# Two weight loads made whole, x loaded in two halves, and the final copy and store split over two engines and two queues, in a one-core decode layer

## The chip, the cores and the metric

The kernel runs on one core of one Trainium2 chip. The metric is the device time of one execution in microseconds (us). Lower is better. Single executions of the kernel before ran from 138.02 to 138.56 us, so differences below 0.3% need several executions, and each comparison below used 5 or 6 of the tried kernel and 6 to 11 of the kernel before, on the same chip. Different experiments ran on different chips.

A ratio in this document is the mean time of one kernel's runs divided by the mean of the other's from the same rounds, with a 95% interval in brackets. It is therefore not quite the ratio of the medians that are quoted beside it.

## The reference

One decode step of a transformer layer, for a batch of 4 with one token each, in bf16:

```python
x = A_x                                   # (4, 1, 1024)
h = x + attn(layernorm(x))                # wq 1024x4096, KV cache: last 2048 of 8192 positions,
                                          # 32 query heads, 4 KV heads, Dh 128; wo 4096x1024
h2 = h + (silu(n @ w1) * (n @ w3)) @ w2   # n = layernorm(h); w1, w3 1024x3584, w2 3584x1024
return h2
```

Almost all the bytes are weights and cache: wq 8.4 MB, K and V 8.4 MB each, wo 8.4 MB, and w1, w3 and w2 7.3 MB each, together 55.6 MB that must come from HBM once.

## The kernel before

All big loads go through one queue (SyncE's) into one ring of SBUF memory, in a fixed plan. Each load is issued as soon as the program order and the ring space allow it. The scheduler of the kernel language places the semaphore waits. This is the part that the change touches, with cuts marked:

```python
plan = [
    ("wq", load_rows, (0, wq_v, N_Q, 0, 4)),            # first half of wq
    ("wq", load_rows, (32 * KIB, wq_v, N_Q, 4, 4)),     # second half
    ("k", ...), ("k", ...), ("v", ...), ("v", ...), ("wo", ...), ("w1", ...),
    ("w3", load_rows, (0, w3_v, N_F, 0, 4)),            # first half of w3
    ("w3", load_rows, (28 * KIB, w3_v, N_F, 4, 4)),     # second half
    ("w2", ... 17 rows), ("w2", ... 7), ("w2", ... 3), ("w2", ... 1),
]
nc.scalar.dma_start(out=x_sb[:], in_=x_flat)            # x, 4 rows of 2 KB, ScalarE's queue
# ... cut: four more small loads of x in another layout (x_q), ScalarE's queue
# ... cut: layer norm, q = x wq, K transposes and scores, softmax, PV, wo
for i in range(IO):                                     # wo, 32 rows
    # ... matmuls of row i
    if i == 11:
        load_next()                                     # second half of w3
# ... cut: layer norm, w1, silu, w3
for i in range(IF):                                     # w2 accumulates on h in y2_ps (one PSUM bank)
    # ... 4 matmuls of row i
res = act.tile([P, CG], BF16)                           # 128 x 256
nc.scalar.copy(out=res[:], in_=y2_ps[:])
nc.scalar.dma_start(out=out_flat.rearrange("b (j c) -> j b c", j=JG), in_=res[0:P:RS, :])
```

## Time and profile before

| | before |
|---|---|
| median device time (first three runs) | 138.23 us (138.06 to 138.29) |
| span in the profile | 136.3 us |
| bytes read from HBM | 55.59 MB |
| share of the span in which the load queue's packets keep the 16 DMA engines busy | 95.3% |
| TensorE (PE) busy | 50% |

The slice table cuts the span into 40 slices of 3.4 us; each digit is the busy share of the DMA engines in tenths.

```profile
DMA  5999899999999999997988989989799999989960
```

The load stream has no hole from about 3 us to 133 us. The chain that ended last, followed back from the end, says the same by engine and by line:

```profile
DMA 58%; PE 21%; ACT 13%; DVE 5%; issue 1%; SPq 0%; ACTq 0%
DMA ring<-in_B_w_dram 42%; DMA ring<-in_A_wq_dram 16%; PE kt_ps L263 9%; ACT kT L269 6%; PE scores_ps L248 5%; ACT z L304 3%; PE q_ps L215 2%; PE g_ps L403 2%; DVE rmax L280 2%; ACT Pm L285 2%; PE OT_ps L326 2%; DVE pT L294 1%; DVE z L300 1%; ACT L285 1%; DVE q_sb L225 1%
```

Now the timeline. The columns are start in us, length in us, engine, line, operation, output and inputs, shape, count, and in brackets the idle time before it and what ended it. A name ending in q (ACTq, SPq) is an engine's sequencer, here issuing a DMA. First the start of the kernel:

```profile
2.52 1.27 DVE L158 BATCH_NORM_STATS2 stats<-x_sb 4x6 f32<-4x512 bf16 x2
...
13.05 3.58 PE L215 MATMUL q_ps<-ring,xnT 128*4 128x512 bf16 x32 [6.05 <-DMA ring<-in_A_wq_dram]
...
22.55 3.15 PE L215 MATMUL q_ps<-ring,xnT 128*4 128x512 bf16 x32 [5.92 <-DMA ring<-in_A_wq_dram]
...
27.45 2.03 PE L263 MATMUL kt_ps<-ident,ring 128*128 128x128 bf16 x33
```

The first half of wq lands and 32 matmuls run at 13.05; the other 32 run at 22.55, when the second half is there. Then K starts. Here is the rest of the weights and the tail:

```profile
107.50 3.13 PE L403 MATMUL u_ps<-ring,hnT 128*32 128x448 bf16 x32 [3.00 <-DMA ring<-in_B_w_dram]
...
115.98 3.17 PE L403 MATMUL u_ps<-ring,hnT 128*32 128x448 bf16 x32 [5.34 <-DMA ring<-in_B_w_dram]
...
120.33 1.70 DVE L425 STREAM_TRANSPOSE hgT<-hg 128x896 bf16<-128x896 bf16 x1
...
126.30 3.82 PE L433 MATMUL y_ps<-ring,hgT 128*32 128x256 bf16 x68 [7.14 <-DMA ring<-in_B_w_dram]
...
132.38 0.92 PE L433 MATMUL y_ps<-ring,hgT 128*32 128x256 bf16 x16 [0.71 <-DMA ring<-in_B_w_dram]
...
133.35 0.37 ACT L443 CAST res<-y_ps 128x256 bf16<-128x256 f32 x1 [26.54 <-PE y_ps L433]
133.75 0.61 ACTq L444 DMA_DIRECT2D out_dram<-res  x1
```

Every weight matmul is released by a load ("<-DMA"). Between the end of hgT (122.0) and the first w2 load (126.3) there are 4.3 us of slack. After the last load comes the only part that nothing hides: four matmuls, a 0.37 us copy, a store.

### The profile page before, as it was taken

To read this page: it belongs to the slowest core of one execution; us is meant where nothing else is said; L and a number is where in the kernel's file an instruction comes from. 1 tells how busy PE (TensorE), PEld (TensorE's weight loads), DVE (VectorE), ACT (ScalarE), POOL (GpSimd) and SP (SyncE) were. 2 spreads that over 40 slices of the span, in tenths; PEclk is the share of its full clock that TensorE was granted. 3 is DMA by queue.
4 is the path that set the end of the run, shared out by engine and by line. 5 is a ranking of instruction groups with operands and counts; after the bars stand their busy time and mean duration, and the time that the engine had idled before them with its cause. 6 is when DMAs were issued, how large, how long until landed. Compare 5 with 4: busy or idle time off the path is not lost.

```text
span 136.3 us, 2302 instructions
## 1 busy us (share of the span) xinstructions
PE 67.9 (50%) x1035; PEld 42.9 (31%) x1035; DVE 42.6 (31%) x73; ACT 31.0 (23%) x36; POOL 1.7 (1%) x8
## 2 busy tenths in 40 slices
PE   0101803698989889105259538830096440900960
PEld 0100201274656565001149427610043210300840
DVE  6440000244444444609940030160000695070000
ACT  0400000155555646092944000000003300000001
POOL 5000000000000000000000000000000000000000
PEclk9999999999999999965555865897557777555577
DMA  5999899999999999997988989989799999989960
GB/s 156 462 462 443 385 413 418 423 447 423 428 437 409 437 437 423 435 582 341 538 385 365 524 365 442 459 353 522 328 412 463 434 437 447 429 388 409 426 261 5
DMA packets 2662, 55.75 MB, mean 409 GB/s; under 512 B 312, under 2 KB 344, under 8 KB 604
## 3 DMA queue, kind: packets, MB, share of 16 engines
q1 hardware_dynamic: 2592, 55.58, 95.3%
q8 instruction: 8, 0.13, 0.3%
q10 hardware_dynamic: 60, 0.02, 0.1%
q14 instruction: 2, 0.02, 0.0%
HBM read 55.59 MB, written 0.01 MB: 408 GB/s over the span
## 4 chain that ended last, share of the span: by engine, by line
DMA 58%; PE 21%; ACT 13%; DVE 5%; issue 1%; SPq 0%; ACTq 0%
DMA ring<-in_B_w_dram 42%; DMA ring<-in_A_wq_dram 16%; PE kt_ps L263 9%; ACT kT L269 6%; PE scores_ps L248 5%; ACT z L304 3%; PE q_ps L215 2%; PE g_ps L403 2%; DVE rmax L280 2%; ACT Pm L285 2%; PE OT_ps L326 2%; DVE pT L294 1%; DVE z L300 1%; ACT L285 1%; DVE q_sb L225 1%
## 5 line engine op out<-in xcount | busy, mean ns | idle before, releaser
L269 ACT COPY kT<-kt_ps 128x1024 bf16<-128x1024 bf16 x16 | 15.8, 1014 | 12.0 <-PE kt_ps L263 12.0
L263 PE MATMUL kt_ps<-ident,ring 128*128 128x128 bf16 x256 | 16.4, 219 | 0.0
L263 PEld LDWEIGHTS <-ring 128*128 128x128 bf16 x256 | 14.3, 98 | 5.0 <-issue 4.9
L267 DVE COPY kT<-kt_ps 128x1024 bf16<-128x1024 bf16 x16 | 11.1, 691 | 15.2 <-PE kt_ps L263 15.2
L215 PE MATMUL q_ps<-ring,xnT 128*4 128x512 bf16 x64 | 6.7, 596 | 12.0 <-DMA ring<-in_A_wq_dram 12.0
L403 PEld LDWEIGHTS <-hnT 128*32 128x32 bf16 x128 | 5.3, 137 | 23.1 <-issue 20.5
L248 PE MATMUL scores_ps<-kT,qz 128*32 128x512 bf16 x64 | 9.9, 609 | 3.1 <-ACT kT L269 3.1
L326 PE MATMUL OT_ps<-z,ring 128*128 128x32 bf16 x256 | 7.4, 185 | 6.7 <-ACT z L304 5.0
L403 PE MATMUL u_ps<-ring,hnT 128*32 128x448 bf16 x64 | 6.3, 572 | 8.3 <-DMA ring<-in_B_w_dram 8.3
L403 PE MATMUL g_ps<-ring,hnT 128*32 128x448 bf16 x64 | 5.4, 525 | 9.0 <-DMA ring<-in_B_w_dram 9.0
L433 PE MATMUL y_ps<-ring,hgT 128*32 128x256 bf16 x112 | 5.7, 370 | 8.4 <-DMA ring<-in_B_w_dram 8.3
L326 PEld LDWEIGHTS <-ring 128*128 128x128 bf16 x256 | 7.3, 103 | 7.4 <-issue 7.4
L433 PEld LDWEIGHTS <-hgT 128*32 128x32 bf16 x112 | 4.4, 129 | 10.3 <-issue 6.1
L215 PEld LDWEIGHTS <-xnT 128*4 128x4 bf16 x64 | 2.1, 116 | 16.2 <-issue 15.9
L353 PE MATMUL y_ps<-ring,o 128*32 128x256 bf16 x128 | 5.8, 365 | 2.0 <-DMA ring<-in_A_wo_dram 2.0
L443 ACT CAST res<-y_ps 128x256 bf16<-128x256 f32 x1 | 0.4, 372 | 26.5 <-PE y_ps L433 26.5
L304 ACT ACTIVATE z<-pt_ps,mask 128x512 bf16<-128x512 f32 x8 | 5.3, 687 | 3.5 <-DVE z L300 3.5
L225 DVE TENSOR_SCALAR q_sb<-q_ps 128x512 bf16<-128x512 f32 x1 | 0.7, 690 | 17.2 <-PE q_ps L215 17.2
L353 PEld LDWEIGHTS <-o 128*32 128x32 bf16 x128 | 4.8, 130 | 3.8 <-issue 3.1
L300 DVE TENSOR_SCALAR z<-pt_ps,mask 128x512 bf16<-128x512 f32 x8 | 5.5, 740 | 1.2 <-ACT z L304 0.8
L296 PE MATMUL pt_ps<-pT,perm 128*128 128x512 bf16 x4 | 2.4, 607 | 6.8 <-DVE pT L294 6.8
L417 DVE RECIPROCAL eg<-eg 128x896 f32<-128x896 f32 x1 | 5.8, 5753 | 0.0
(73 smaller groups left out, 40.5 us busy)
## 6 DMA issues: line engine op xcount, KB each, us to landing
ring<-in_A_wq_dram SPq DMA_DIRECT2D x2, 4096.0 KB, 16.8
ring<-in_A_k_cache_dram SPq DMA_DIRECT2D x4, 2048.0 KB, 25.5
ring<-in_A_v_cache_dram SPq DMA_DIRECT2D x4, 2048.0 KB, 40.2
ring<-in_B_w_dram SPq DMA_DIRECT2D x1, 7168.0 KB
ring<-in_B_w_dram SPq DMA_DIRECT2D x2, 3584.0 KB, 28.6
ring<-in_B_w_dram SPq DMA_DIRECT2D x1, 4352.0 KB
ring<-in_B_w_dram SPq DMA_DIRECT2D x1, 1792.0 KB
ring<-in_B_w_dram SPq DMA_DIRECT2D x1, 768.0 KB
```

Of the source, the lines that this page charges most:

```text
L215: nc.tensor.matmul(q_ps[QD * g : QD * g + B, hf * 512 : (hf + 1) * 512], lhsT=xnT[:, kc, :], rhs=wq_t[:, c0 : c0 + 512], start=(kc == 0), ...
L248: nc.tensor.matmul(scores_ps[QD * g : QD * (g + 1), n * 512 : (n + 1) * 512], lhsT=qz[:, b, g * QD : (g + 1) * QD], rhs=kT_v[:, g, :, :], ...
L263: nc.tensor.transpose(out=kt_ps[:, jj, :], in_=k_v[:, n * NJ + t * TB + jj, :], identity=ident[:])
L267: nc.vector.tensor_copy(out=kT[:, t * TB : (t + 1) * TB, :], in_=kt_ps[:])
L269: nc.scalar.copy(out=kT[:, t * TB : (t + 1) * TB, :], in_=kt_ps[:])
L300: nc.vector.tensor_scalar(out=z[:, :, g, :], in0=pt_ps[:], scalar1=mask[:, g : g + 1], scalar2=None, op0=ALU.mult)
L304: nc.scalar.mul(out=z[:, :, g, :], in_=pt_ps[:], mul=mask[:, g : g + 1])
L326: nc.tensor.matmul(OT_ps[:, b, :], lhsT=loaded["v"][b][:, j, :], rhs=PTz[j // NJ][:, (j % NJ) * B + b, :, :], start=(j == 0), stop=(j == J ...
L353: nc.tensor.matmul(y_ps[QD * j : QD * (j + 1), :], lhsT=o4[:, i, :, :].rearrange("p b s -> p (b s)"), rhs=loaded["wo"][i][:, j * CG : (j + ...
L403: nc.tensor.matmul(out_ps[QD * j : QD * (j + 1), hf, :HF], lhsT=hnT[:, k, :], rhs=loaded[kind][k][:, c0 : c0 + HF], start=(k == 0), stop=( ...
L417: nc.vector.reciprocal(out=eg[:], in_=eg[:])
L433: nc.tensor.matmul(y2_ps[QD * j : QD * (j + 1), :], lhsT=hgT[:, i, :], rhs=loaded["w2"][i][:, j * CG : (j + 1) * CG], start=False, stop=(i ...
```

## The change

The intent: fewer and larger loads for wq and w3, and a shorter tail, by splitting the last copy over VectorE and ScalarE by columns and storing each part from its own queue. x is also loaded as two column halves, so that the layer norm statistics can begin on the first. The core of the diff:

```diff
-        ("wq", load_rows, (0, wq_v, N_Q, 0, 4)),
-        ("wq", load_rows, (32 * KIB, wq_v, N_Q, 4, 4)),
+        ("wq", load_rows, (0, wq_v, N_Q, 0, 8)),
 ...
-        ("w3", load_rows, (0, w3_v, N_F, 0, 4)),
-        ("w3", load_rows, (28 * KIB, w3_v, N_F, 4, 4)),
+        ("w3", load_rows, (0, w3_v, N_F, 0, 8)),       # issued after wo's row 12
 ...
-    nc.scalar.dma_start(out=x_sb[:], in_=x_flat)
+    for c0, c1 in ((0, 512), (512, D)):
+        nc.scalar.dma_start(out=x_sb[:, c0:c1], in_=x_flat[:, c0:c1])
 ...
-    nc.scalar.copy(out=res[:], in_=y2_ps[:])
-    nc.scalar.dma_start(out=out_flat.rearrange("b (j c) -> j b c", j=JG), in_=res[0:P:RS, :])
+    out_v = out_flat.rearrange("b (j c) -> j b c", j=JG)
+    CV = 160
+    nc.vector.tensor_copy(out=res[:, :CV], in_=y2_ps[:, :CV])
+    nc.scalar.copy(out=res[:, CV:], in_=y2_ps[:, CV:])
+    nc.sync.dma_start(out=out_v[:, :, :CV], in_=res[0:P:RS, :CV])
+    nc.scalar.dma_start(out=out_v[:, :, CV:], in_=res[0:P:RS, CV:])
```

(The calls that issue the next load were moved to fit; they are cut here.)

More of the change, by code (lines that the diff above doesn't have):

```diff
@@ L136 @@
     x_sb = act.tile([B, D], BF16)
-    nc.scalar.dma_start(out=x_sb[:], in_=x_flat)
-    load_next(5)
+    for c0, c1 in ((0, 512), (512, D)):
+        nc.scalar.dma_start(out=x_sb[:, c0:c1], in_=x_flat[:, c0:c1])
+    load_next(4)
     ident = const.tile([P, P], BF16)
@@ L221 @@
                 )
-        if kc == RQ - 1:
-            load_next()
+    load_next()
     q_sb = act.tile([P, CQ], BF16)
@@ L332 @@
             )
-        if b % BS == BS - 1:
+        if b == BS - 1:
             load_next()
```

## The prediction

> **What bounds the kernel now.** The load stream. The profile's slice table shows the DMA engines 8 to 10 tenths busy from 3 to 133 us; the windows view gives 426 to 430 GB/s in the wq and K stages. In the timeline the weight matmuls start when loads land: wq halves at 13.05 and 22.55 us, wo 82.25, w1 99.06, w3 halves 107.50 and 115.98, w2 126.30, 130.55, 132.38, 133.0. Then come four matmuls, a 0.37 us ScalarE copy and the store (issue 0.61 us), ending at 136.3.
>
> **What the change does.**
>
> 1. Bytes, and so stream time, stay the same. One load instead of two saves about 0.4 us of issue, already hidden. Gain: 0.
>
> 2. wq whole: the 32 matmuls that ran at 13.05 (3.58 us) now wait until 22.5. All 64 take about 6.4 us, to 28.9 (before 25.7). In the built order 16 K transposes now precede the q transposes, hiding the q copies: K starts at about 29, not 27.45. K, softmax and PV come 1.5 to 3 us later. w1's load is issued when half of PV is done: 73.2 becomes 75 to 76. The queue has wo to move until about 80 (lands 82.25, less an estimated 2 us of completion), so it stays fed. The third K load now waits for all of wq (22.5, not 13.05); two K loads (10 us) are queued by then.
>
> 3. PV's result comes at about 83 instead of 81; wo matmuls (5.8 us) and layer norm (4.2 us) end at about 94, still ahead of w1 at 99.
>
> 4. w3 whole is issued after wo's row 12, at 85 to 87; w1 keeps the queue busy to about 97. But all 64 w3 matmuls start at about 116 and take 5.4 to 6.3 us (before: 3.17 us after the second half). hg and hgT (1.09, 1.70 us) end at about 125 instead of 122.05; w2's first piece lands at 126.3. 1 to 2 us of 4.2 us slack are left.
>
> 5. Final copy: in the built program ScalarE's part waits for VectorE's. Both read one PSUM bank (the Trainium skill, "PSUM — Partial Sum Buffer", section on bank collisions, says engines can't access one bank of a partition in the same cycle; no run here shows that yet). Estimate from the trace's copies (VectorE 0.29 us at 128 columns, 0.42 at 256; ScalarE 0.27 and 0.37): 0.32 + 0.05 + 0.24 = 0.61 us against 0.37. The second store is issued 0.2 us later, and the second queue gains nothing (the skill, "DMA: Bandwidth & Descriptors", "Issuing engines are not separate DMA queues": all run on the same 16 engines). Cost: +0.2 us.
>
> **On the critical path** lies only point 5; 2 to 4 eat slack. From 138.23 us I predict 138.4 us, range 137.9 to 139.3. Faster by over 2%: 2%; within 2%: 95%; slower: 3%.
>
> **What would show it.** Right: last w2 landing at 133 us, give or take 0.4; no hole in the DMA share; q matmuls one block of about 6.4 us from 22.5; w3 matmuls one block at 116; w2 matmuls released by the load; ScalarE's res copy after VectorE's. Wrong: a hole in the load stream near 80 or 97 us (2, 4); the first w2 matmul released by hgT (4); the copies overlapping (5).
>
> **What would make it wrong.** A lower granted TensorE clock (0.5 in many windows after 62 us) stretching PV or the w3 block beyond their slack; stores under 512 bytes a row (320 and 192) completing more slowly; a different load rate with 64 KB rows per partition than with 32 KB.

## More of the kernel before

The store's packets, in the DMA view of the window from 134.4 to 135.45 us, are 20 packets on ScalarE's queue (q10) and nothing else:

```profile
DMA  0000000000000000000000022221000000000000
...
q10 hardware_dynamic: 20, 0.01, 2.9%
```

## The result, and the profile after

| | before | after |
|---|---|---|
| median device time | 138.19 us (138.04 to 138.40, 6 runs) | 138.94 us (138.75 to 139.17, 6 runs) |
| ratio | | 1.0055, 95% interval 1.0041 to 1.0068 |
| span in the profile | 136.3 us | 137.0 us |

The change costs 0.75 us. That lies inside the predicted range (137.9 to 139.3) and counts as "within 2%", but the predicted cost was only 0.2 us. The rest of this document is about the other 0.55 us.

The slice table and the chain after. The stream is as full as before:

```profile
DMA  9797996999999999999979999989989989997940
```

```profile
DMA 56%; PE 25%; ACT 11%; DVE 4%; issue 1%; ACTq 0%; SPq 0%
DMA ring<-in_B_w_dram 40%; DMA ring<-in_A_wq_dram 16%; PE kt_ps L261 10%; PE scores_ps L246 6%; ACT kT L267 5%; PE q_ps L214 5%; ACT z L302 3%; PE g_ps L401 2%; DVE rmax L278 2%; ACT Pm L283 2%; PE OT_ps L324 1%; DVE pT L292 1%; DVE z L298 1%; ACT L283 1%; PE qt_ps L227 1%
```

The start after the change, as a timeline:

```profile
10.44 0.68 DVE L157 BATCH_NORM_STATS2 stats<-x_sb 4x6 f32<-4x512 bf16 x1 [7.41 <-DMA x_sb<-in_A_x_dram]
...
22.68 6.44 PE L214 MATMUL q_ps<-ring,xnT 128*4 128x512 bf16 x64 [9.54 <-DMA ring<-in_A_wq_dram]
...
29.05 0.84 PE L261 MATMUL kt_ps<-ident,ring 128*128 128x128 bf16 x12
```

The 64 matmuls of wq now form one block of 6.44 us at 22.68, and K starts at 29.05 instead of 27.45. A surprise off the critical path: the statistics of x's second half start only at 10.44 us, because that 4 KB load had not landed before. The tail after the change:

```profile
82.70 1.65 PE L324 MATMUL OT_ps<-z,ring 128*128 128x32 bf16 x55 [4.15 <-issue]
...
86.15 5.46 PE L351 MATMUL y_ps<-ring,o 128*32 128x256 bf16 x128 [0.82 <-DVE o L340]
...
99.12 5.35 PE L401 MATMUL g_ps<-ring,hnT 128*32 128x448 bf16 x64 [5.46 <-DMA ring<-in_B_w_dram]
...
116.05 5.43 PE L401 MATMUL u_ps<-ring,hnT 128*32 128x448 bf16 x64 [11.57 <-DMA ring<-in_B_w_dram]
...
122.65 1.70 DVE L423 STREAM_TRANSPOSE hgT<-hg 128x896 bf16<-128x896 bf16 x1
...
126.31 3.82 PE L431 MATMUL y_ps<-ring,hgT 128*32 128x256 bf16 x68 [4.83 <-DMA ring<-in_B_w_dram]
...
132.37 0.90 PE L431 MATMUL y_ps<-ring,hgT 128*32 128x256 bf16 x16 [0.76 <-DMA ring<-in_B_w_dram]
...
133.32 0.32 DVE L443 CAST res<-y_ps 128x160 bf16<-128x160 f32 x1 [8.97 <-PE y_ps L431]
133.67 0.69 SPq L445 DMA_DIRECT2D out_dram<-res  x1
133.68 0.24 ACT L444 CAST res<-y_ps 128x96 bf16<-128x96 f32 x1 [26.89 <-DVE res L443]
134.08 0.62 ACTq L446 DMA_DIRECT2D out_dram<-res  x1
```

The w3 matmuls are one block from 116.05, hgT ends at 124.35, and the w2 matmuls are still released by the load, at 126.31 (before: 126.30), and the last 16 at 132.37 (before: 132.38). So in these profiles everything up to the last load takes the same time. The whole difference comes after it. ScalarE's copy starts only after VectorE's has ended. And in the DMA view of the same window as before, something new is in the way:

```profile
DMA  0000000000009000000000111000000000001100
...
q14 instruction: 1, 0.01, 3.1%
q1 hardware_dynamic: 20, 0.01, 2.1%
q10 hardware_dynamic: 15, 0.00, 1.2%
```

Queue q14 is an instruction queue: one packet of instructions (8,192 bytes, 525 ns in the packet records) runs at 134.74 us, and the stores' packets (q1 and q10) run from 134.97 us.

The tail can be read as a sum of four terms, worked out from the packet and semaphore records of each trace and from the device time of the profiled run: A from the end of the last load packet to the issue of the last store; B from there until that store has landed; C from there to the end of the span; D the device time less the span. In us:

```text
kernel                  last load    A     B     C     D    sum A..D   device
before                   132.67    1.08  1.75  0.84  1.78    5.45     138.12
after                    132.60    1.47  2.05  0.84  1.87    6.23     138.83
```

This sum is better to compare than single times: in seven profiles of kernels whose loads are those of the kernel before, the end of the last load packet varied from 132.67 to 132.98 us, while the sum of a second profile of the kernel before came out at 5.42. The change added 0.39 in A, 0.30 in B and 0.09 in D. Only about 0.24 of A was predicted.

### The profile page after: what moved, and what is told of

Its sections match the earlier page's. It is cut to its first block, busy times and chain, and to the rows that moved or that the text cites. A ratio compares the mean times of both kernels' runs of the same rounds, so it can differ in the third digit from the quotient of the medians.

```text
span 137.0 us, 2303 instructions
## 1 busy us (share of the span) xinstructions
PE 67.0 (49%) x1035; PEld 42.0 (31%) x1035; DVE 42.7 (31%) x74; ACT 31.0 (23%) x36; POOL 1.7 (1%) x8
## 4 chain that ended last, share of the span: by engine, by line
DMA 56%; PE 25%; ACT 11%; DVE 4%; issue 1%; ACTq 0%; SPq 0%
DMA ring<-in_B_w_dram 40%; DMA ring<-in_A_wq_dram 16%; PE kt_ps L261 10%; PE scores_ps L246 6%; ACT kT L267 5%; PE q_ps L214 5%; ACT z L302 3%; PE g_ps L401 2%; DVE rmax L278 2%; ACT Pm L283 2%; PE OT_ps L324 1%; DVE pT L292 1%; DVE z L298 1%; ACT L283 1%; PE qt_ps L227 1%
## 5 line engine op out<-in xcount | busy, mean ns | idle before, releaser
L261 PE MATMUL kt_ps<-ident,ring 128*128 128x128 bf16 x256 | 17.1, 220 | 0.0
L246 PE MATMUL scores_ps<-kT,qz 128*32 128x512 bf16 x64 | 10.5, 609 | 2.6 <-ACT kT L267 2.6
L401 PE MATMUL u_ps<-ring,hnT 128*32 128x448 bf16 x64 | 5.4, 523 | 11.6 <-DMA ring<-in_B_w_dram 11.6
L171 PE MATMUL tp_ps<-ident,xn 4*128 4x4 bf16 x8 | 0.7, 199 | 12.5 <-DVE xn L164 12.5
```

The costliest lines, as they stand in the source:

```text
L246: nc.tensor.matmul(scores_ps[QD * g : QD * (g + 1), n * 512 : (n + 1) * 512], lhsT=qz[:, b, g * QD : (g + 1) * QD], rhs=kT_v[:, g, :, :], ...
L261: nc.tensor.transpose(out=kt_ps[:, jj, :], in_=k_v[:, n * NJ + t * TB + jj, :], identity=ident[:])
L401: nc.tensor.matmul(out_ps[QD * j : QD * (j + 1), hf, :HF], lhsT=hnT[:, k, :], rhs=loaded[kind][k][:, c0 : c0 + HF], start=(k == 0), stop=( ...
```

## The experiments

Theory at first: all of the 0.75 us lies in the copies and stores, and the loads cost nothing. Rival: the whole loads, with their larger packets, cost part of it.

### Only the loads changed

```diff
  (wq, w3 and x_sb loaded as in the changed kernel; final copy and store as before)
```

> The changed loads (wq, w3, x_sb) with the old final copy and single store. Theory T (all of the +0.75 us lies after the last load): 138.1 to 138.3 us, ratio 1.000 give or take 0.001; last w2 landing at 133.0. Rival L (whole wq and w3, or their 64 KB and 56 KB packets, cost part of it): 138.45 us or more, with the last landing or the last w2 matmul later than in the kernel before.

Measured: 138.62 us against 138.12; ratio 1.0026 (1.0012 to 1.0041). Something in the load part costs about 0.36 us (difference of the means), which the theory did not allow. But the sum of its tail is 5.68, not 5.45, although its tail's code is that of the kernel before. The last load packet ended at 132.81, within the spread of the other profiles, so the later landing that the rival named is not seen.

### Only the tail changed

```diff
-    nc.scalar.copy(out=res[:], in_=y2_ps[:])
-    nc.scalar.dma_start(out=..., in_=res[0:P:RS, :])
+    (two copies and two stores, as in the changed kernel)
```

> The loads of the kernel before with the new final copies and two stores. Theory T: 138.85 to 139.05 us, ratio 1.0045 to 1.006, all of the change's cost. Rival L: clearly less, 138.3 to 138.6.

Measured: 138.51 us against 138.12; ratio 1.0025 (1.0011 to 1.0039). So the tail costs about 0.39 us, and the first theory fell: the tail alone is not all, and the two halves of the change add up to the whole (0.36 + 0.39 against 0.75). Its timeline:

```profile
133.64 0.32 DVE L445 CAST res<-y_ps 128x160 bf16<-128x160 f32 x1 [11.31 <-PE y_ps L433]
133.99 0.69 SPq L447 DMA_DIRECT2D out_dram<-res  x1
134.00 0.24 ACT L446 CAST res<-y_ps 128x96 bf16<-128x96 f32 x1 [26.98 <-DVE res L445]
134.26 0.61 ACTq L448 DMA_DIRECT2D out_dram<-res  x1
```

ScalarE's copy waits for VectorE's, as predicted. Its store is issued 0.03 us after its copy ends (before rounding). In the changed kernel that gap was 0.16 us, with the same code.

### Within the tail: two copies, one store

```diff
-    nc.scalar.copy(out=res[:], in_=y2_ps[:])
+    nc.vector.tensor_copy(out=res[:, :160], in_=y2_ps[:, :160])
+    nc.scalar.copy(out=res[:, 160:], in_=y2_ps[:, 160:])
     nc.scalar.dma_start(out=out_v, in_=res[0:P:RS, :])
```

> Split copies (VectorE, then ScalarE waiting for it), then one store of whole 512-byte rows from ScalarE's queue. Theory C: store issued 0.3 to 0.35 us later, 138.5 to 138.6. If C were all of it: 138.9. If the serial copies cost nothing: 138.2.

Measured: 138.40 us against 138.12; ratio 1.0018 (1.0005 to 1.0030), 0.24 us by the means.

```profile
133.48 0.33 DVE L445 CAST res<-y_ps 128x160 bf16<-128x160 f32 x1 [11.43 <-PE y_ps L433]
133.84 0.24 ACT L446 CAST res<-y_ps 128x96 bf16<-128x96 f32 x1 [27.89 <-DVE res L445]
134.11 0.61 ACTq L447 DMA_DIRECT2D out_dram<-res  x1
```

The copies take 0.60 us from the start of the first to the end of the second, against 0.37 before, and term A grows from 1.08 to 1.30. This is the part of the cost that the prediction named, at its predicted size (0.24 us). The run's own expectation, a store 0.3 to 0.35 us later, was too high: A grew by 0.2 us.

### Within the tail: one copy, two stores

```diff
     nc.scalar.copy(out=res[:], in_=y2_ps[:])
-    nc.scalar.dma_start(out=..., in_=res[0:P:RS, :])
+    nc.sync.dma_start(out=out_v[:, :, :160], in_=res[0:P:RS, :160])
+    nc.scalar.dma_start(out=out_v[:, :, 160:], in_=res[0:P:RS, 160:])
```

> One ScalarE copy as before, then the two column stores (320 and 192 bytes a row) from two queues. Theory S (the second store and the narrow rows cost about half, as the longer time from last packet to completion in the profile suggests): 138.4 to 138.7. Rival C (only the serial copies cost): 138.2.

Measured: 138.62 us against 138.12; ratio 1.0032 (1.0019 to 1.0045), 0.44 us by the means.

```profile
133.52 0.37 ACT L445 CAST res<-y_ps 128x256 bf16<-128x256 f32 x1 [27.53 <-PE y_ps L433]
133.91 0.69 SPq L446 DMA_DIRECT2D out_dram<-res  x1
133.92 0.61 ACTq L447 DMA_DIRECT2D out_dram<-res  x1
```

Both stores are issued at the same moment, no later than before, yet term B is 2.08 instead of 1.75: two stores issued together complete later than one. The packet records show where: ScalarE's packets move from 135.17 to 135.29 us, 1.25 us after the issue as in the kernel before, and SyncE's only from 135.53, after them. SyncE's queue is not slow by itself: in tail_only, where its store was issued first, it landed 1.77 us after its issue. Term C is 0.94 instead of 0.84; its cause comes up below.

### Two stores by rows

```diff
     nc.scalar.copy(out=res[:], in_=y2_ps[:])
-    nc.scalar.dma_start(out=..., in_=res[0:P:RS, :])
+    nc.sync.dma_start(out=out_v[0:2], in_=res[0:64:RS, :])      # every row keeps 512 bytes
+    nc.scalar.dma_start(out=out_v[2:4], in_=res[64:P:RS, :])
```

> One ScalarE copy as before, two stores from two queues, split by rows, so that every row keeps its 512 bytes. Theory R (rows under 512 bytes are what made the two column stores cost 0.44 us): 138.1 to 138.3. Rival Q (a second store costs by itself, through its second issue and completion): 138.4 to 138.6.

Measured: 138.55 us against 138.21; ratio 1.0024 (1.0012 to 1.0036), 0.32 us by the means; term B 1.97, term C again 0.94. The second store costs by itself, without narrow rows: about 0.2 us in B and 0.1 us in C. Whether narrow rows add a little (0.44 against 0.32 us) these runs cannot tell.

In the changed tail the two stores are issued 0.27 us apart (tail_only), and then B is 1.81: the cost of a second store and the cost of the serial copies overlap, so the two do not simply add.

### Which load costs? A control, and each load change alone

```text
(no edit: the kernel before, built again)
```

> The kernel before, unchanged, as a control. If the timing of two builds of one program is comparable to about 0.1%, this gives 138.0 to 138.3 us and a ratio of 1.000 give or take 0.001. Theory N (the 0.36 us of the load changes is spread between executions or builds, not a cost): a ratio up to 1.002 here too. Its profile also gives a second reading of the end of the load stream.

Measured: 138.22 us against 138.14; ratio 0.9999 (0.9987 to 1.0011). Two builds of one program compare to about 0.1%. Their profiles differ in one place that matters below. Within PV, TensorE stood still for 1.68 us in the profile of the kernel before:

```profile
77.67 1.54 PE L326 MATMUL OT_ps<-z,ring 128*128 128x32 bf16 x55 [1.68 <-issue]
```

In the profile of before_again, the same program, it stood still for 3.91 us at the same matmul:

```profile
80.34 1.65 PE L326 MATMUL OT_ps<-z,ring 128*128 128x32 bf16 x55 [3.91 <-issue]
```

```diff
-        ("wq", load_rows, (0, wq_v, N_Q, 0, 4)),
-        ("wq", load_rows, (32 * KIB, wq_v, N_Q, 4, 4)),
+        ("wq", load_rows, (0, wq_v, N_Q, 0, 8)),
```

> Only wq as one load. Theory W (the whole wq, with its 64 KB packets at the start of the stream, is what cost 0.36 us of the load changes): 138.4 to 138.6. Otherwise 138.1 to 138.25.

Measured: 138.33 against 138.14; ratio 1.0013 (0.9999 to 1.0027). Not resolved from zero (0.18 us by the means, between the run's two expectations); its tail's sum is 5.47.

```diff
-        ("w3", load_rows, (0, w3_v, N_F, 0, 4)),
-        ("w3", load_rows, (28 * KIB, w3_v, N_F, 4, 4)),
+        ("w3", load_rows, (0, w3_v, N_F, 0, 8)),       # issued after wo's row 12
```

> Only w3 as one load, issued after wo's row 12. Theory X (the whole w3 costs): 138.4 to 138.6. Otherwise 138.1 to 138.25, with one block of w3 matmuls at about 116 and the w2 matmuls still released by the load.

Measured: 138.13 against 138.14; ratio 0.9993 (0.9981 to 1.0005). The whole w3 costs nothing.

```diff
-    nc.scalar.dma_start(out=x_sb[:], in_=x_flat)
+    for c0, c1 in ((0, 512), (512, D)):
+        nc.scalar.dma_start(out=x_sb[:, c0:c1], in_=x_flat[:, c0:c1])
```

> Only x_sb as two column loads. Theory Y (it costs): 138.4 or more. Otherwise 138.1 to 138.25. In the profile: if a small transfer's packets take turns with the large ones on their engine, then with wq's 32 KB packets (about 1.2 us each) the second half's BatchNorm statistics start at 6 to 8 us, between 2.5 (one load, kernel before) and 10.4 (behind 64 KB packets, changed kernel).

Measured: 138.50 us against 138.14; ratio 1.0022 (1.0010 to 1.0034), 0.31 us by the means. So the culprit among the loads is the smallest of them, the 8 KB load of x cut in two. The side question was answered as expected:

```profile
7.88 0.68 DVE L159 BATCH_NORM_STATS2 stats<-x_sb 4x6 f32<-4x512 bf16 x1 [4.77 <-DMA x_sb<-in_A_x_dram]
```

With 32 KB packets in the stream the second half's statistics start at 7.88 us, with 64 KB packets (the changed kernel) at 10.44. The packet records show why: behind 32 KB packets the small packets on an engine follow each other at steps of about 1.23 us, behind 64 KB packets at about 2.44 us. That is about the length of one large packet record, 1.21 and 2.42 us. The Trainium skill, "DMA: Bandwidth & Descriptors", section "Queues, rings and completion order", says that each engine goes round-robin between its queues, one packet at a time. These traces agree on the turns: one small record goes for each large one. That a packet typically holds 9 to 17 descriptors, as the page also says, they do not show. This was not on the critical path: the wq matmuls wait for wq until 22.7 us anyway.

### A theory about small packets, which fell

The new theory (P): small packets, on the few engines that carry x, put those engines behind, and the slowest engine sets the end of the stream. If so, fewer small packets must help.

```diff
-    for j in range(JG):
-        nc.scalar.dma_start(out=x_q[QD * j : QD * (j + 1) : RS, :], in_=x_flat[:, j * CG : ...])
+    nc.scalar.dma_start(out=x_q[0:P:RS, :], in_=x_flat.rearrange("b (j c) -> j b c", j=JG))
```

> x_q by one load in place of four: the same 16 rows, with 3 fewer completion packets on each of the few DMA engines that carry them. Theory P (small packets, each taking a turn on a few engines, put those engines behind, and the slowest engine sets the end of the stream): 0.05 to 0.15 us less than before; the spread between first and last engine at the end of wq's first half shrinks from 0.5 us to 0.3 to 0.45. Rival (the count of small packets has no effect): 138.1 to 138.25.

Measured: 138.40 us against 138.21; ratio 1.0017 (1.0006 to 1.0029). Slower, which neither the theory nor its rival expected.

```diff
-    (no x_q loads)                h1 = y_ps + x_q
+    for j in range(JG):           # x added by four selector matmuls ahead of wo's
+        nc.tensor.matmul(y_ps[QD * j : QD * (j + 1), :], lhsT=sel[:], rhs=x_sb[:, ...], start=True, stop=False)
```

> No x_q loads at all: the residual is added by four selector matmuls in front of wo's. Theory P: the spread between first and last engine at the end of wq's first half falls from 0.5 to under 0.2 us, and the time to 137.7 to 138.0 (0.2 to 0.45 us less than before). Rival (small packets have no effect on the end of the stream): 138.1 to 138.3.

Measured: 138.62 us against 138.21; ratio 1.0029 (1.0017 to 1.0041). Theory P fell as an account of the time. In its one profile the spread between the first and the last engine at the end of wq's first half was smaller (0.38 us; 0.43 to 0.67 in the profiles with four x_q loads and wq in halves), but the stream is not shown to end earlier for it: the last load ended at 132.59, and in w3_only, which keeps those loads, at 132.58. The tail grew, although no line of it was touched:

```text
kernel           A     B     C     D    sum     ScalarE instructions   waits after the store   8 KB fetch at
before         1.08  1.75  0.84  1.78  5.45          68                       1                135.79
before_again   1.05  1.75  0.84  1.78  5.42          68                       1                135.72
xsb_only       1.05  1.80  0.93  1.89  5.67          69                       2                134.72
loads_only     1.13  1.78  0.89  1.88  5.68          69                       2                134.58
xq_one_load    1.09  1.74  1.03  1.78  5.65          65                       4                137.41
xq_on_pe       1.13  1.77  1.09  1.92  5.90          64                       5                137.73
```

(The instructions are counted in the built program; the waits and the fetch, that is, the start of the packet on q14, are read from the trace.) Two things move with changes that seem unrelated to the tail.

- At the end, SyncE waits for every DMA semaphore in a fixed order of five instructions, each for one or two semaphores. There are eight such semaphores, given out in turn, so a DMA more or less at the start changes which one the final store gets. If the store's stands late in the order, the other waits are over by then; if it stands early, they follow one by one after the store has landed, about 0.065 us each. C grows from 0.84 (one wait) to 1.09 (five).
- A packet of 8,192 bytes on the instruction queue q14 moves with the number of instructions in ScalarE's program. With 68 (eight traces) it starts after the last store has landed; with 69 (four traces) it starts 0.64 to 0.66 us after the start of ScalarE's store instruction, which takes 0.62 to 0.63 us, that is, as soon as ScalarE is past it. The instructions in the traces say the same: in 12 of the 14 traces exactly 64 of ScalarE's had started when this packet started (65 in tail_only; xq_on_pe's trace has only 63). With 68 in the program the 64th is one of the instructions that close the program, with 69 it is the store.

### The deciding run: one spare ScalarE instruction

If the position in ScalarE's program decides it, the loads can be left as they were, and one idle instruction on ScalarE must turn the tail_only kernel into one as slow as the whole change.

```diff
  (tail_only, and:)
+    spare = act.tile([B, 1], FP32)
+    nc.scalar.copy(out=spare[:], in_=rstd[:])     # 4 x 1, early in the kernel, used by nothing
```

> The loads of the kernel before, the new copies and two stores, and one spare 4x1 ScalarE copy early on, so that ScalarE's program has 69 instructions as in the changed kernel (68 in the kernel before and in tail_only). No load is changed. Theory Z (the 0.3 us that the load changes seemed to cost is the one more instruction on ScalarE: the 8 KB fetch that the trace shows on an instruction queue moves from after the store to 134.7 us, where it collides with the store): 138.75 to 139.0 us, ScalarE's store issued 0.1 to 0.2 us after its copy ends, the fetch near 134.7, the time outside the span 1.87 instead of 1.78. Rival V (the second x_sb load itself, as a load, costs): 138.45 to 138.65 as in tail_only, fetch after the store, 1.78 outside the span.

Measured: 138.97 us against 138.20; ratio 1.0053 (1.0039 to 1.0067), the same as the whole change (1.0055) within the noise. Theory Z holds. First, for comparison, the queues (packets, MB, share of the window) that moved anything in tail_only between 134.4 and 135.45 us:

```profile
q1 hardware_dynamic: 20, 0.01, 2.1%
```

There, only SyncE's store moves packets, and no q14; ScalarE's store moves its packets after this window, and the q14 packet comes at 136.42 us. Then the timeline of tail_plus_act2:

```profile
133.39 0.33 DVE L447 CAST res<-y_ps 128x160 bf16<-128x160 f32 x1 [11.54 <-PE y_ps L435]
133.74 0.69 SPq L449 DMA_DIRECT2D out_dram<-res  x1
133.75 0.24 ACT L448 CAST res<-y_ps 128x96 bf16<-128x96 f32 x1 [26.26 <-DVE res L447]
134.15 0.62 ACTq L450 DMA_DIRECT2D out_dram<-res  x1
```

And its DMA view of the same window:

```profile
q14 instruction: 1, 0.01, 2.8%
q1 hardware_dynamic: 20, 0.01, 2.1%
q10 hardware_dynamic: 6, 0.00, 0.6%
```

The store is issued 0.16 us after ScalarE's copy has ended (133.99 to 134.15; in tail_only 0.03), and the q14 packet is there, at 134.80 for 465 ns. The four sums side by side:

```text
kernel                      A     B     C     D    sum    device of the profiled run
before                    1.08  1.75  0.84  1.78  5.45    138.12
tail_only                 1.28  1.81  0.88  1.78  5.75    138.73
tail_plus_act2            1.44  1.96  0.88  1.87  6.15    138.86
after                     1.47  2.05  0.84  1.87  6.23    138.83
```

One spare instruction adds 0.16 to A, 0.15 to B and 0.09 to D, 0.40 us together; by the means of the timed runs it is 0.33 us (0.72 less 0.39 over the kernel before). Each of these two has an interval of about 0.19 us either way, and they come from different chips, so the 0.33 is uncertain by about 0.27 (an estimate from those two). The last load packet ended at 132.71, within the spread, so the spare instruction did not act through the load stream. With it, no cost of the load changes is left to explain beyond the noise.

No version beat the kernel before: w3_only is equal to it (0.9993), all others are slower.

### What stays open

That the extra instruction causes the delay is shown. How is only partly shown. In B the packet records show a part: in the changed kernel SyncE's store has four data packets that start at 135.26 to 135.31 while the others were through by 135.09, and that gap ends with the q14 packet at 135.26. In tail_plus_act2 it is the same: four packets at 135.26 to 135.31, and the q14 packet ends at 135.27. Why ScalarE issues its store 0.16 us after its copy (A), before the q14 packet even starts, why the landing came 0.57 us after the last packet instead of 0.32, and why 0.09 us more passes outside the span (D), the records do not say. The late issue does not come with every such packet: in xsb_only and loads_only, with one store, the store is issued 0.03 and 0.05 us after its copy, and what their tails gain is mostly in C (0.09 and 0.05) and D (0.11 and 0.10). That the q14 packet is ScalarE's own instruction fetch is concluded from its timing and from its moving with ScalarE's instruction count (between tail_only and tail_plus_act2 no other engine's program changed in length); no field of the trace names its owner. No run took x_sb's second load away from ScalarE while keeping it as a load.

## Why the prediction was right or wrong

- Point 1, "Bytes, and so stream time, stay the same": right. The last 16 w2 matmuls start at 132.37 (before 132.38).
- Point 2, wq: right. The block is 6.44 us (predicted 6.4), K starts at 29.05 (29), the third K load is issued at 22.65 (22.5), and w1's load at 75.78 (75 to 76). No hole in the stream.
- Point 3, "PV's result comes at about 83": off by 3 us. wo's matmuls were released by PV's result at 86.15. TensorE stood still for 4.15 us within PV, without a wait that the profile shows ("issue"), where it had stood 1.68 us before. The change did not cause that: the control build stood still for 3.91 us there, and the 14 traces range from 1.31 to 4.15. In all of them the standstill ended 2.2 to 2.4 us after the start of a 16,384-byte packet on instruction queue q8, so it looks like a wait for TensorE's own instructions, which no run tested. The predicted shift itself was right: the 153 matmuls ahead of the standstill start 2.55 us later (71.75 before, 74.30 after). It cost only slack: the layer norm ended at 95.9, before w1 at 99.12.
- Point 4, w3: right in what matters. One block from 116.05, 5.43 us long; hgT ended at 124.35, 1.96 us before the w2 load. The w3 load was issued about 2 us later than predicted (89.0), since wo's matmuls were late, and the stream still stayed full.
- Point 5, the tail: the mechanism was right, the size wrong. "ScalarE's part waits for VectorE's" held (0.60 us for both, predicted 0.61). The Trainium skill's statement in "PSUM — Partial Sum Buffer" on bank collisions fits what the scheduler did, but no run tried simultaneous reads. "The second queue gains nothing" also held, as the skill's "DMA: Bandwidth & Descriptors", section "Issuing engines are not separate DMA queues", suggested, and more: the second store costs 0.32 to 0.44 us when issued together with the first, 0.10 us of it in C. The step that failed is the sum "Cost: +0.2 us", that is, 138.23 to 138.4. It held only the longer copies. Missing were the completion of a second store (0.15 us by the timed runs, 0.39 for the whole tail less 0.24 for the copies; of it the traces show 0.06 in B and 0.04 in C of tail_only, where it overlaps with the copies) and the delay that one more instruction on ScalarE brings, in the changed kernel x_sb's second load (0.33 us by the timed runs). The split of x_sb was not costed in the prediction at all. That the measured time lies inside the predicted range is in part luck: the range was 1.4 us wide, and the larger of the two missing terms was in none of its reasons.
- "What would make it wrong" named slow completion of narrow rows. Completion was indeed slower, but two stores of full 512-byte rows were slower too, so narrow rows are not needed to explain it.

## What to carry to other kernels

Behind a load stream that is full to the end, as here, what comes after the last byte is what counts, so write it as a sum (copy, issue, landing, final waits, time outside the span) and cost every term: two stores from two queues took longer than one, and a copy split over two engines out of one PSUM bank ran one after the other. An added instruction or DMA far from the tail can move an instruction fetch, or the order of the final waits, into the tail; here that was worth 0.2 to 0.4 us, as much as the effects under study. For effects of that size run a control build and a build with one idle instruction before believing that a change of loads was the cause.

## What the Trainium skill lacked or had wrong

- "Runtime: NRT & Kernel Launch", section "Instruction fetch mechanics", calls the cost of crossing an instruction block "mostly hidden" and gives blocks of 16 KiB. In these traces instruction queue q8 (by its timing TensorE's) does move packets of 16,384 bytes, eight of them, but q14's is 8,192 bytes, and when one fell on the final store it was not hidden: one idle ScalarE instruction cost 0.33 us (0.72 less 0.39 over the kernel before, by the means). Nor does it look hidden in PV, where TensorE stood still for 1.31 to 4.15 us, until 2.2 to 2.4 us after one of q8's packets began.
- "DMA: Bandwidth & Descriptors", section "Issuing engines are not separate DMA queues", says that several issuing engines only save issue time. For a final 8 KB store it was worse than that: two stores issued together cost 0.32 us (by rows) and 0.44 us (by columns) more than one, 0.10 us of each in the final waits.
- The same page, section "Queues, rings and completion order", gives the turn-taking by packet but not what it means for a small load beside a large one: the step was 1.23 us with 32 KB packets and 2.44 us with 64 KB packets, and a 4 KB load issued by 1.7 us was usable only at 7.9 us (behind 32 KB packets) and 10.4 us (behind 64 KB).
- No page has the final waits for DMA semaphores: their order in the closing wait list moved the end by 0.25 us (C from 0.84 to 1.09).
